# Products of values in tiles of 64 rows by 32 columns, into two banks of PSUM, beside two single score banks instead of three

## The chip, the cores and the metric

The kernel runs on one core of one Trainium2 chip. The metric is device time in microseconds (us) for one execution; a core's engines work side by side and wait for each other by semaphores. PE is the matmul engine (its weight loads are listed apart as PEld), ACT the scalar engine, DVE the vector engine, POOL the GpSimd engine, and SP issues most DMAs. Matmul results go to PSUM, which has eight banks of 128 partitions by 512 fp32 numbers each.

## What is computed

Two sublayers work on 2048 rows of 512 numbers, and a gate mixes them. Only the first, attention with 32 heads of 16 numbers each, matters for the change:

```python
q, k, v = qkv[0], qkv[1], qkv[2]
scores = einsum("bhqd,bhkd->bhqk", q, k) * Dh ** -0.5
p = softmax(scores, axis=-1)
o = einsum("bhqk,bhkd->bhqd", p, v)
a = o.transpose(0, 2, 1, 3).reshape(B, S, D) @ wo
out = g * a + (1 - g) * b
```

Here b is a Fourier sublayer (two products with DFT matrices along the features and along the rows), and g is a sigmoid of a weighted row sum.

## The kernel before

**The whole.** The order on every engine is written out by hand in the program. A front part (projections, the values `va`, most of the Fourier products) comes first; beside it go "scans", score products whose only use is the row maximum. Then follows the attention loop of 512 steps (lines 991 to 1039), and a short tail (from line 1045).

**A step of attention.** The 32 heads go as 16 pairs `p`. For each pair there are two halves `h` of 1024 queries and 16 blocks `kb` of 128 keys: 16 x 2 x 16 = 512 steps. A step makes scores for two heads (j = 0, 1) and two blocks of 512 queries (c = 0, 1), in fp32r (`qk`, line 204). The two heads of a call lie on rows 0 to 49 and 64 to 113 of the operands, so that their two products stand in the upper and the lower half of the array at the same time, with 128 columns each.

- c = 0 goes to a double bank, `wide1` (`qk_both`, line 229). One ACT instruction of 1024 numbers per partition makes the exponentials `eb` of both heads (line 234). There is one such double bank, so the next step's call waits until ACT has read it.
- c = 1 goes to two single banks (`qk_single`, line 237), from a rotation `order_` of three: d0, d1, k0. Two ACT instructions of 512 numbers make `e`, head 1 first (lines 241 and 242). Then line 243 swaps the last two names of the rotation. With three banks this gives head 1 the same bank in every step, while head 0 takes the other two in turn.
- The other double bank, `wide0`, belongs to what is done beside: in the first 300 steps a scan (line 135) whose maximum DVE takes at once (line 137), and later the rest of the Fourier and output products (line 185, "fill" here).

**The products of values** (`pv`, line 753) come one step later. The exponentials (128 keys by 512 queries) stream against 17 columns of `va`: 16 numbers of the head and a column of ones, which gives the sum for the softmax. Both are fp32, which the profile lists as two matmuls and two weight loads for each one of the program. Four tiles of 128 rows by 32 columns (`tile_position=(0, r)`) stand side by side in the array, one each for (c, j). All add into one bank, `pvb` (its tag is k1), over the 16 steps of a half. At the end of a half `quotients` (line 762) copies `pvb` to SBUF on DVE and sends the sums off; `divide` does the rest later. The next half's first product of values waits for that copy.

**The order on PE.** In the first 300 steps ("scan stage" here): scores c = 0, scan, scores c = 1, products of values of the step before. From step 301 (`MIX`, line 47; "fill stage") the products of two steps are made together in every second step. A period of two steps is then: scores c = 0 and c = 1, products of two steps, scores c = 0 and c = 1, fill products.

**PSUM.** `wide0` and `wide1` take two banks each, and the four tags d0, d1, k0, k1 one each: all eight banks are used.

**The tail** reads the last half out of `pvb` with two copies of 256 columns, one on DVE and one on ACT (lines 1050 and 1051), transposes them in the array, divides, and ends with the last output products; it uses the single banks too.

Of the kernel before, what the change touches and what calls it, by code (L numbers as in the profile page):

```python
# [24 lines left out]
NB = S // P  # L25
ND = D // P
NC = S // 512
VC = DH + 1
# [25 lines left out]
def build(tc, xT, wqkv, wo, wrT, wiT, cr, ci, gate, out):  # L54
    nc = tc.nc
    with ExitStack() as ctx:
# [21 lines left out]
        va = keep.tile([P, NB, H, VC], F32, name="va")  # L78
# [47 lines left out]
        def scan(n, ps):  # L126

            p, i = SEQ[n]
            qb, c = i // 4, i % 4
            qs, ks = scanned[p]  # L130
            if i == 0:
                new_maxima(p)
            for j in range(2):
                b = 64 * j
                nc.tensor.matmul(ps[:, j, :], qs[b:b + 48, qb * P:(qb + 1) * P],  # L135
                                 ks[b:b + 48, c * 512:(c + 1) * 512], start=True, stop=True)
            nc.vector.tensor_reduce(mx[p][:, :, qb, c], ps, axis=AX.X, op=ALU.max)  # L137
# [54 lines left out]
        def wide(i, name):  # L192
            return psf.tile([P, 2, 512], F32, tag=f"wide{i}", name=name)
# [16 lines left out]
                nc.tensor.matmul(pss[j], ks[b:b + 50, kb * P:(kb + 1) * P],  # L210
                                 qs[b:b + 50, q0:q0 + 512], start=True, stop=True)

        psk, order_ = [], ["d0", "d1", "k0"]

        def narrow(tag, name):
            return psk[0].tile([P, 512], F32, tag=tag, name=name)
# [6 lines left out]
        def next_eb():  # L223
            if len(both) < 4:
                both.append(ring4.tile([P, 2, 512], F32, tag="c", name="eb"))
            ebs[0] += 1
            return both[(ebs[0] - 1) % 4]

        def qk_both(p, h, kb):

            ps = wide(1 - SCANS_IN, "s3")
            qk(p, h, kb, 0, [ps[:, j, :] for j in range(2)])
            e = next_eb()
            nc.scalar.activation(e, ps, AF.Exp, scale=SCALE)  # L234
            return [e[:, j, :] for j in range(2)]

        def qk_single(p, h, kb, e):

            pss = [bank() for j in range(2)]
            qk(p, h, kb, 1, pss)  # L240
            for j in (1, 0):
                nc.scalar.activation(e[j], pss[j], AF.Exp, scale=SCALE)  # L242
            order_[-2:] = order_[-1], order_[-2]
            return e

        ebs, ahead, sums = [0], [], []
# [4 lines left out]
        with ExitStack() as pf:  # L251
# [381 lines left out]
            with ExitStack() as py:  # L633
# [13 lines left out]
                def go_ahead(k):  # L647

                    if k == 0:
                        assert seen[0] == FRONT, (seen, pace)  # L650
                        scanned.update(unfolded)
                        sums.append(narrow("k1", "pvb"))
                        nc.vector.memset(sums[0], 0.0)
                    if k == 1:
                        e = next_eb()
                        ahead.append(qk_single(0, 0, 0, [e[:, j, :] for j in range(2)]))
                    elif k == 2:
                        scan(seen[0], wide(1 - SCANS_IN, "s1"))
                        seen[0] += 1
                    else:  # L660
                        ahead.append(qk_both(0, 0, k // 3))
# [8 lines left out]
                for n, (ph, t, u) in enumerate(coef):  # L670
# [33 lines left out]
                    for w in range(CS):  # L704
                        s = u * CS + w
                        for i, (c_, a_) in enumerate(((hi, ah[s]), (hi, al[s]), (lo, ah[s]))):
                            halves_of(pss[t], c_[:, w, :], a_, s == 0 and i == 0, s == NB - 1 and i == 2)
                            beside()
                            if n >= len(coef) - NU and 3 * s + i in AHEAD:
                                go_ahead(AHEAD.index(3 * s + i))  # L710
                        if swap:
                            if 3 <= s < 8:
                                early[s + 5] = load_operand(1, s + 5, cp)
                            after(1 + 5 * (s % 8) + 4 * (s // 8), renew, s)
# [15 lines left out]
        with ExitStack() as pa:  # L730
# [1 line left out]
            cw = pa.enter_context(tc.tile_pool(name="cw2", bufs=2, reuse_waits="tile"))  # L732
            ap = pa.enter_context(tc.tile_pool(name="ap", bufs=1, reuse_waits="tile"))

            pvb = sums[0]
            rb = ap.tile([P, 512], F32, name="rb")
            nc.gpsimd.memset(rb, 1.0)

# [7 lines left out]
            def qk2(p, h, kb, c):  # L746
                if c == 0:
                    return qk_both(p, h, kb)
                n = turn1[0]
                turn1[0] += 1  # L750
                return qk_single(p, h, kb, [ring[n % len(ring)] for ring in single])

            def pv(p, h, kb, es):
                for c, j, r in quads:
                    nc.tensor.matmul(pvb[r:r + VC, :], va[:, kb, 2 * p + j, :], es[c][j],  # L755
                                     start=kb == 0, stop=kb == NB - 1, tile_position=(0, r))

            def bank2():
                ps = wide(1 - SCANS_IN, "s3")
# [2 lines left out]
            def quotients(p, h):  # L762
                ob = ap.tile([P, 512], F32, tag="ob", name="ob", bufs=2)
                nc.vector.tensor_copy(ob, pvb)  # L764
                lc = sm.tile([P, 16], F32, tag="lc", name="lc")
                for n, (c, j, r) in enumerate(quads):
                    nc.gpsimd.dma_start(lc[32 * n:32 * n + 32, :],  # L767
                                        ob[r + DH:r + VC, :].rearrange("p (s e) -> p s e", e=16))
                return p, h, ob, lc
# [189 lines left out]
            def part(t, *ks):  # L959

                if t not in groups:
                    if t in (3, 9):
                        ps = pair_banks()
                        groups[t] = ps[:, 0, :], ps[:, 1, :]
                    else:
                        groups[t] = bank2() if t == 8 else (bank(), pvb if t == 11 else bank())
                for k in ks:
                    mix_rest(t, groups[t], k, k == 0 or 7 < t < 11, k == 2)
# [5 lines left out]
            def flush():  # L974
                done = pend.pop(0)
                pv(*done)
                return done
# [13 lines left out]
            for step in range(NP * PERIODS):  # L991
                p, i = step // PERIODS, step % PERIODS
                h, kb = i // NB, i % NB
# [19 lines left out]
                es = ahead[2:] if step == 1 else [qk2(p, h, kb, 0)]  # L1013
# [18 lines left out]
                if done and done[2] == NB - 1:  # L1032
                    halved.append((step + (10 if done[0] < NP - 2 else 7 if done[0] < NP - 1 else 3), quotients(*done[:2])))
# [11 lines left out]
            halves_ = [slice(0, 256), slice(256, 512)]  # L1045
            blocks_ = [slice(s * P, (s + 1) * P) for s in range(4)]
            ob = ap.tile([P, 512], F32, tag="ob", name="ob", bufs=2)
            oh, ol = (cw.tile([P, 512], F32R, tag=tag, name=tag) for tag in ("chi", "clo"))
            direct[1].append((oh, ol))
            for c, copy in zip(halves_, (nc.vector.tensor_copy, nc.scalar.copy)):  # L1050
                copy(ob[:, c], pvb[:, c])
            part(3, 1)
            turned, spread = bank(), bank()
            for q in blocks_:
# [61 lines left out]
```

## Time and profile before

| what | value |
|---|---|
| median of 3 runs | 1726.87 us (1726.72 to 1727.06) |
| profiled execution, first to last instruction (span) | 1725.2 us |
| PE busy | 1713.5 us, 99% |
| ACT busy | 1506.8 us, 87% |
| DVE busy | 1089.1 us, 63% |
| POOL busy | 648.7 us, 38% |
| mean granted clock of PE | 0.999 |

Of the profiled execution only the span is given; it lies 1.7 us below the median of the runs, which count what lies around the instructions as well. Times within the trace are in us from the span's start. In a row of the timeline stand the start, how long the record (or the merged records) lasted, engine, line, operation, tiles as out<-in, shape (rows*columns for PE) and count; in brackets stands how long the engine had been idle before it, and what ended that. A record of PE lasts longer than the array is taken by it, since matmuls follow each other in a pipeline: it is the steps from start to start that add up. So PE's 99% doesn't say that the array streamed for 99% of the time.

### The profile page before, as it was taken

To read this page: it belongs to the slowest core of one execution; us is meant where nothing else is said; L and a number is where in the kernel's file an instruction comes from. 1 tells how busy PE (TensorE), PEld (TensorE's weight loads), DVE (VectorE), ACT (ScalarE), POOL (GpSimd) and SP (SyncE) were. 2 spreads that over 40 slices of the span, in tenths; PEclk is the share of its full clock that TensorE was granted. 3 is DMA by queue.
4 is the path that set the end of the run, shared out by engine and by line. 5 is a ranking of instruction groups with operands and counts; after the bars stand their busy time and mean duration, and the time that the engine had idled before them with its cause. 6 is when DMAs were issued, how large, how long until landed. Compare 5 with 4: busy or idle time off the path is not lost.

```text
span 1725.2 us, 36082 instructions
## 1 busy us (share of the span) xinstructions
PE 1713.5 (99%) x13680; PEld 1044.7 (61%) x13680; DVE 1089.1 (63%) x2059; ACT 1506.8 (87%) x2489; POOL 648.7 (38%) x770
## 2 busy tenths in 40 slices
PE   9999999999999999999999999999999999999998
PEld 7888888988888885333333333333455555555554
DVE  6898888999999996666666666666512212122333
ACT  6447889888888888999999999999988888888886
POOL 3672436655555762223233242322322322223222
PEclk9999999999999999999999999999999999999999
DMA  7783557534337663243323342351334244265712
GB/s 257 241 285 75 156 158 211 158 112 115 103 111 211 153 136 72 37 73 58 66 59 67 54 82 44 58 107 37 65 80 94 72 110 91 67 150 139 175 36 101
DMA packets 123710, 193.03 MB, mean 112 GB/s; under 512 B 54112, under 2 KB 56656, under 8 KB 116624
## 3 DMA queue, kind: packets, MB, share of 16 engines
q1 hardware_dynamic: 84464, 170.20, 37.7%
q0 software_dynamic: 38496, 19.47, 5.7%
q8 instruction: 107, 1.75, 0.4%
q10 hardware_dynamic: 576, 1.05, 0.2%
q14 instruction: 67, 0.55, 0.1%
HBM read 129.63 MB, written 61.61 MB: 111 GB/s over the span
## 4 chain that ended last, share of the span: by engine, by line
PE 96%; DVE 2%; DMA 1%; issue 1%; ACT 0%; SPq 0%; DVEq 0%; POOL 0%; ACTq 0%; POOLq 0%
PE pvb L755 29%; PE xy L185 25%; PE s L210 19%; PE s L185 9%; PE s L154 9%; PE s L135 5%; DVE fold L160 1%; DMA q_d<-eh 0%; DMA raws<-wqkv 0%; DMA ks<-kf_d 0%; PE s L554 0%; DVE y L853 0%; ACT fold L158 0%; DVE s L278 0%; DVE b L334 0%
## 5 line engine op out<-in xcount | busy, mean ns | idle before, releaser
L234 ACT ACTIVATE eb<-s 128x1024 f32<-128x1024 f32 x512 | 578.7, 1130 | 65.4 <-PE s L210 65.4
L242 ACT ACTIVATE e<-s 128x512 f32<-128x512 f32 x1022 | 608.9, 709 | 0.4 <-PE s L210 0.4
L137 DVE TENSOR_REDUCE mx<-s 128x2 f32<-128x1024 f32 x364 | 441.4, 1224 | 188.7 <-PE s L135 188.5
L755 PE MATMUL pvb<-eb,va 128*17 128x512 f32 x2052 | 513.0, 597 | 0.0
L755 PE MATMUL pvb<-e,va 128*17 128x512 f32 x2044 | 512.1, 597 | 0.0
L160 DVE CUSTOM_DVE_ANT_0 fold<-s,fold 128x512 f32<-128x512 f32 x660 | 443.9, 690 | 52.7 <-PE s L154 24.4
L158 ACT ACTIVATE fold<-s 128x512 f32<-128x512 f32 x660 | 389.9, 603 | 73.3 <-PE s L154 52.3
L210 PEld LDWEIGHTS s<-qs,ks 50*128 50x128 f32 x2048 | 214.9, 184 | 355.2 <-ACT eb L234 255.1
L210 PE MATMUL s<-qs,ks 50*128 50x512 f32 x2048 | 420.0, 434 | 0.0
L185 PE MATMUL xy<-b,c 64*128 64x512 f32 x2448 | 397.3, 392 | 0.3 <-ACT c L333 0.3
L154 PE MATMUL s<-ks,qs 48*128 48x512 f32 x1320 | 315.3, 405 | 1.6 <-DVE mx L160 1.0
L185 PEld LDWEIGHTS xy<-b,c 64*128 64x128 f32 x2448 | 283.9, 187 | 17.6 <-issue 1.0
L154 PEld LDWEIGHTS s<-ks,qs 48*128 48x128 f32 x1320 | 172.9, 184 | 47.0 <-DVE mx L160 12.5
L774 POOL DMA_DIRECT2D r_d<-lc x31 | 18.1, 583 | 456.4 <-DVE lc L773 456.4
L755 PEld LDWEIGHTS pvb<-eb,va 128*17 128x17 f32 x2052 | 70.5, 96 | 189.9 <-issue 182.7
L135 PE MATMUL s<-ks,qs 48*128 48x512 f32 x728 | 151.6, 394 | 0.7 <-DVE mx L137 0.7
L767 POOL DMA_DIRECT2D lc<-ob x124 | 62.9, 514 | 156.3 <-DVE ob L764 156.1
L185 PE MATMUL xy<-w,b 64*128 64x512 f32 x768 | 115.3, 392 | 0.0
L365 POOL TENSOR_TENSOR c<-craw,c 128x512 fp32r<-128x512 f32 x84 | 109.4, 1302 | 6.7
L185 PE MATMUL s<-b,chi 64*128 64x512 f32 x670 | 105.4, 391 | 0.0
L364 POOL CAST c<-craw 128x512 fp32r<-128x512 f32 x84 | 53.3, 635 | 125.1 <-PE xy L185 120.1
L871 DVE CAST chi<-craw 128x512 fp32r<-128x512 f32 x40 | 19.1, 477 | 111.4 <-PE s L185 99.3
(136 smaller groups left out, 1535.2 us busy)
## 6 DMA issues: line engine op xcount, KB each, us to landing
qs<-q_d SPq DMA_DIRECT2D x66, 256.0 KB
craw<-ci SPq DMA_DIRECT2D x64, 256.0 KB
craw<-cr SPq DMA_DIRECT2D x60, 256.0 KB
ks<-k_d SPq DMA_DIRECT2D x44, 256.0 KB
qs<-q_d SPq DMA_DIRECT2D x66, 128.0 KB
ab_d<-ab SPq DMA_DIRECT2D x32, 256.0 KB
y_d<-y SPq DMA_DIRECT2D x32, 256.0 KB
o_d<-oh POOLq DMA_DIRECT2D x28, 256.0 KB, 13.8
```

The lines of the kernel that those rows point to most:

```text
L135: nc.tensor.matmul(ps[:, j, :], qs[b:b + 48, qb * P:(qb + 1) * P], ks[b:b + 48, c * 512:(c + 1) * 512], start=True, stop=True)
L137: nc.vector.tensor_reduce(mx[p][:, :, qb, c], ps, axis=AX.X, op=ALU.max)
L154: nc.tensor.matmul(ps, qs[b:b + 48, qb * P:(qb + 1) * P], ks[b:b + 48, c * 512:(c + 1) * 512], start=True, stop=True)
L158: nc.scalar.activation(fold[j], ps, AF.Relu)
L160: nc.vector.tensor_tensor_reduce(out=fold[j], in0=ps, in1=fold[j], scale=1.0, scalar=-3.0e38, op0=ALU.add, op1=ALU.max, accum_out=mx[p][:, ...
L185: nc.tensor.matmul(ps[j], lhs[r], rhs[r], start=first, stop=last)
L210: nc.tensor.matmul(pss[j], ks[b:b + 50, kb * P:(kb + 1) * P], qs[b:b + 50, q0:q0 + 512], start=True, stop=True)
L234: nc.scalar.activation(e, ps, AF.Exp, scale=SCALE)
L242: nc.scalar.activation(e[j], pss[j], AF.Exp, scale=SCALE)
L365: sub(lo, raw, hi.bitcast(F32))
L755: nc.tensor.matmul(pvb[r:r + VC, :], va[:, kb, 2 * p + j, :], es[c][j], start=kb == 0, stop=kb == NB - 1, tile_position=(0, r))
L767: nc.gpsimd.dma_start(lc[32 * n:32 * n + 32, :], ob[r + DH:r + VC, :].rearrange("p (s e) -> p s e", e=16))
```

## The change

`pv` cuts each product in two by rows. Instead of four tiles of 128 rows by 32 columns there are eight of 64 rows by 32 columns: rows 0 to 63 (the first 64 keys) add into `pvb`, and rows 64 to 127 into a second bank `pvc`, so that each (c, j) has a tile in each half of the array. The program's products of values are twice as many. `pvc` takes the tag k0, which leaves the rotation: `qk_single` has two banks, d0 and d1. With the swap of line 243, head 0 of a step then takes the bank that head 1 had in the step before, and head 1 the bank that head 0 had, which ACT reads last. `quotients` adds `pvc` with a second DVE instruction, and the first product of the next half into `pvc` waits for that. At the start both banks are set to zero. In the tail ACT copies both parts of `pvb`, DVE adds `pvc` to each, and k0 then joins the rotation again.

```diff
-        psk, order_ = [], ["d0", "d1", "k0"]
+        psk, order_ = [], ["d0", "d1"]
...
-                        sums.append(narrow("k1", "pvb"))
-                        nc.vector.memset(sums[0], 0.0)
+                        for tag in ("k1", "k0"):
+                            sums.append(narrow(tag, "pvb"))
+                            nc.vector.memset(sums[-1], 0.0)
...
-            pvb = sums[0]
+            pvb, pvc = sums
...
             def pv(p, h, kb, es):
                 for c, j, r in quads:
-                    nc.tensor.matmul(pvb[r:r + VC, :], va[:, kb, 2 * p + j, :], es[c][j],
-                                     start=kb == 0, stop=kb == NB - 1, tile_position=(0, r))
+                    for b, sums_ in ((0, pvb), (64, pvc)):
+                        nc.tensor.matmul(sums_[r:r + VC, :], va[b:b + 64, kb, 2 * p + j, :], es[c][j][b:b + 64, :],
+                                         start=kb == 0, stop=kb == NB - 1, tile_position=(b, r))
...
                 nc.vector.tensor_copy(ob, pvb)
+                nc.vector.tensor_add(ob, ob, pvc)
...
-            for c, copy in zip(halves_, (nc.vector.tensor_copy, nc.scalar.copy)):
-                copy(ob[:, c], pvb[:, c])
+            for c in halves_:
+                nc.scalar.copy(ob[:, c], pvb[:, c])
+                nc.vector.tensor_add(ob[:, c], ob[:, c], pvc[:, c])
+            order_.append("k0")
```

## The prediction

> **What bounds the kernel now.** I read the page first: its busy shares, the chain that ended last, and the costliest groups.
>
> ```profile
> span 1725.2 us, 36082 instructions
> PE 1713.5 (99%) x13680; PEld 1044.7 (61%) x13680; DVE 1089.1 (63%) x2059; ACT 1506.8 (87%) x2489; POOL 648.7 (38%) x770
> ...
> PE pvb L755 29%; PE xy L185 25%; PE s L210 19%; PE s L185 9%; PE s L154 9%; PE s L135 5%; DVE fold L160 1%; DMA q_d<-eh 0%; DMA raws<-wqkv 0%; DMA ks<-kf_d 0%; PE s L554 0%; DVE y L853 0%; ACT fold L158 0%; DVE s L278 0%; DVE b L334 0%
> ...
> L242 ACT ACTIVATE e<-s 128x512 f32<-128x512 f32 x1022 | 608.9, 709 | 0.4 <-PE s L210 0.4
> ```
>
> The products of values (L755) have 29% of a chain that is nearly all PE, so they look like the place to save. But a chain names one engine where two are equally late, so I cut the span into stages: scan stage, fill stage with periods of one length, its last part, tail.
>
> ```profile
> 663.00:1237.00 574.00, 573.28 (x4237) 220.54 (x4235) 387.13 (x358) 571.10 (x904) 166.72 (x251) 1.00 0.32 61
> 1237.00:1593.00 356.00, 356.00 (x2929) 188.72 (x2926) 72.25 (x128) 317.50 (x490) 98.99 (x146) 1.00 0.42 101
> 1593.00:1708.00 115.00, 115.00 (x940) 61.37 (x939) 39.22 (x58) 94.17 (x143) 23.17 (x36) 1.00 0.39 101
> ```
>
> The columns are length, then busy time of PE, PEld, DVE, ACT, POOL. In the scan stage ACT is busy 571.10 of 574.00 us: PE and ACT are both full, so a faster PE gains nothing there. In the fill stage ACT has some 11% free and PE sets the pace. The front, 663 us, isn't touched. One step of the scan stage, PE and ACT:
>
> ```profile
> 1002.66 0.40 PE L135 MATMUL s<-ks,qs 48*128 48x512 f32 x2
> 1002.86 1.15 ACT L234 ACTIVATE eb<-s 128x1024 f32<-128x1024 f32 x1
> 1002.89 0.40 PE L210 MATMUL s<-qs,ks 50*128 50x512 f32 x2
> 1003.22 0.61 PE L755 MATMUL pvb<-eb,va 128*17 128x512 f32 x2
> 1003.23 0.61 PE L755 MATMUL pvb<-e,va 128*17 128x512 f32 x2
> 1003.66 0.60 PE L755 MATMUL pvb<-eb,va 128*17 128x512 f32 x2
> 1003.78 1.21 ACT L242 ACTIVATE e<-s 128x512 f32<-128x512 f32 x2
> 1004.20 0.50 PE L210 MATMUL s<-qs,ks 50*128 50x512 f32 x2
> 1004.54 0.40 PE L135 MATMUL s<-ks,qs 48*128 48x512 f32 x2
> 1004.74 1.17 ACT L234 ACTIVATE eb<-s 128x1024 f32<-128x1024 f32 x1
> ```
>
> On PE a pair of score products takes 0.23 (1002.66 to 1002.89), but 0.33 where the products of values follow (to 1003.22): 0.10 extra. Of these the first pass takes 0.44, the second 0.54 until the next scores: 0.10 extra. And the first scores take 0.34 until the scan instead of 0.23: their weights were not loaded ahead, 0.11. So going to the wide tiles and back costs 0.10 + 0.10 + 0.11 = 0.31 us, and this is what a change of tile shape could save. ACT meanwhile goes from `eb` to `eb` in 1.88 with no idle time in its rows.
>
> **The change part by part.**
>
> *Streaming.* Eight tiles of half the rows stream the same 512 columns in the same two passes: nothing is saved in the passes if all eight run at once. I cost the four more tiles of a pass at 0; the two records of a pass start 0.01 apart (1003.22, 1003.23), so if each further pair of tiles adds as much, it is up to 0.015 x 405 blocks = 6 us.
>
> *The switch between shapes.* Scores use 64 rows by 128 columns, and the products of values now 64 by 32: the row split stays, the column split changes. No row of the trace shows a switch of columns alone. One row shows a switch of rows alone, from transposes (128 by 128) to output products (64 by 128) in the tail:
>
> ```profile
> 1711.48 0.66 PE L1055 MATMUL s<-ident,ob 128*128 128x128 f32 x4
> 1712.06 0.30 PEld L185 LDWEIGHTS s<-b,chi 64*128 64x128 f32 x4 [0.17 <-issue]
> ```
>
> The weight load of the new shape waits for nothing that the profile shows, yet it starts only 0.08 before the last old record ends, and the two switches of both kinds above act alike. So one changed direction is enough for the pause, and I take it that the 0.31 stays (bounds: 0 and 0.31 saved). The Trainium skill, TensorEngine Tiling (Array Packing), Key Properties, says that a change of tiling mode drains the engine while a change of tile doesn't, and its list has 64x128 and 64x32 as two modes. By that rule nothing of the 0.31 goes and the sum is the one below; without it the sum would be that of rival 1. The row above agrees, though only for rows.
>
> *The third score bank.* Now the second score product of a step (head 1, c = 1) needs the bank that head 0 had a step before, which ACT reads last. Until now that wait did not exist. Behind it on PE stand the products of values, and behind these the next c = 0 scores that ACT needs. A closed loop arises. Its links come from the fill stage, where ACT isn't held up by itself:
>
> ```profile
> 1302.22 0.73 PE L210 MATMUL s<-qs,ks 50*128 50x512 f32 x4
> 1302.76 1.03 ACT L234 ACTIVATE eb<-s 128x1024 f32<-128x1024 f32 x1 [0.47 <-PE s L210]
> 1303.68 1.08 ACT L242 ACTIVATE e<-s 128x512 f32<-128x512 f32 x2
> 1304.17 0.65 PE L210 MATMUL s<-qs,ks 50*128 50x512 f32 x4
> 1304.75 0.61 PE L755 MATMUL pvb<-eb,va 128*17 128x512 f32 x2
> 1306.59 0.51 PE L210 MATMUL s<-qs,ks 50*128 50x512 f32 x2
> ...
> 1708.48 1.08 ACT L242 ACTIVATE e<-s 128x512 f32<-128x512 f32 x2
> 1709.61 0.12 PEld L755 LDWEIGHTS pvb<-e,va 128*17 128x17 f32 x4 [0.24 <-ACT e L242]
> ...
> L154 PEld LDWEIGHTS s<-ks,qs 48*128 48x128 f32 x1320 | 172.9, 184 | 47.0 <-DVE mx L160 12.5 <-ACT fold L158 7.5
> ```
>
> Scores c = 0 to the start of `eb`: 0.54 (1302.22 to 1302.76). From there to the end of the last `e`: 2.00 (1303.68 + 1.08 = 1304.76). From an ACT end to PE: 0.05 (1708.48 + 1.08 = 1709.56 to 1709.61). A weight load that stands behind a wait for a bank is held with its product (the L154 row: loads waited for DVE's and ACT's reads), so it is not hidden: 0.11 as above. I take it; without it the term is 0. Then 0.33 to the products of values.
>
> Scan stage: these take 0.98 (1003.22 to 1004.20). Loop over two steps: 0.54 + 2.00 + 0.05 + 0.11 + 0.33 + 0.98 = 4.01, or 2.005 a step.
>
> ```profile
> L234 ACT ACTIVATE eb<-s x290: 1024/1228/1255, 680.4 to 1229.5; 128x1024 f32<-128x1024 f32 x145
> L755 PE MATMUL pvb<-eb,va x648: 592/592/605, 1239.2 to 1590.4; 128*17 128x512 f32 x162
> L234 ACT ACTIVATE eb<-s x48: 1023/1026/1047, 1593.3 to 1707.6; 128x1024 f32<-128x1024 f32 x48
> ```
>
> Now a step takes (1229.5 - 680.4) / 289 = 1.900. So 0.105 x 300 steps = 31.5 us (15 without the weight load, 38 with the late tiles).
>
> Fill stage: the products of two steps take 1.84 (1304.75 to 1306.59). The loop runs once per period, since the scores made after the fill need the bank of those made before it: 0.54 + 2.00 + 0.05 + 0.11 + 0.33 + 1.84 = 4.87. A period now is 1306.59 - 1302.22 = 4.37, and there are 648 / 8 = 81 of them up to 1593. The 24 periods behind (48 `eb` in 114.3 us) are 9.4 us longer than 24 x 4.37; a long one has three fill pairs more, 3 x 0.23 = 0.69, so some 14 are long (5.06, over 4.87: no cost) and 9 short ones add to the 81. 90 x 0.50 = 45 us (35 without the weight load).
>
> *The end of a half.* DVE copies `pvb`, then adds `pvc`; the next half's first product of values waits for both.
>
> ```profile
> 1000.59 0.69 DVE L764 COPY ob<-pvb 128x512 f32<-128x512 f32 x1
>   PEld pvb L755: 6.9, 18
> L607 DVE TENSOR_TENSOR ab<-tx,xy 128x512 f32<-128x512 f32 x20 | 13.7, 683 | 0.0
> ```
>
> The second row says that in the scan stage's 18 halves PE already waits for the copy. An addition with one operand in PSUM is 0.68 (L607), and PE has no slack in the loop: 18 x 0.68 = 12 us (9 if ACT's stock of scores hides a part). Queued behind the addition on DVE is the scan's maximum (1.23 of a 2.0 step), which it delays without making DVE full. In the fill stage the next products come 4.37 - 1.84 = 2.5 us after the last ones, more than copy and addition: 0.
>
> *The ends.* One more memset at the start stands beside fill products: 0. In the tail ACT's and DVE's parts come after each other: 0.5 us.
>
> **Sum:** 31.5 + 12 + 45 + 0.5 = 89 on the span of 1725.2 gives 1814; what lies around it, 1.7 to the median of 1726.87, stays: **1816 us**, 5% slower. Its own range by the bounds is 1786 to 1827.
>
> **The rivals.**
>
> *1. The pauses go, since the row split stays.* Then 0.31 leaves each loop. Scan stage: 4.01 - 0.31 = 3.70, under ACT's 2 x 1.88, so a step stays at 1.90, and the ends of halves cost some 11. Fill stage: 4.87 - 0.31 = 4.56, still over 4.37: 90 x 0.19 = 17; the 14 long ones gain 0.31 each, -4. In all +24: 1751 us. If also the waiting weight load is hidden: 4.45, +7 in place of 17 and 3 less in the scan stage, 1738. If only 0.20 goes: 4.67, +27, -3, +13: 1764. So the gain of PE is eaten by ACT in one stage and by the lost bank in the other. For it: the rows show no switch of columns alone. Against it: the tail's switch. The Trainium skill (TensorE: Matmul & The Clock Gate, Part 3) says that a weight load overlaps a running matmul only where the row group differs; by that the 0.11 stays and this rival is 1764. The row of 1002.66 speaks against such a strict rule: PE goes on to the next pair on the same rows after 0.23, which leaves no room for 0.11 of load.
>
> *2. PE can't do eight tiles at once or can't issue them fast enough.* Instructions in a scan step rise from 28 to 44 (12 for scores and scan, 32 for values), in a period from 72 to 104. The fastest long stretch of the trace is a fill pair, 4 instructions in 0.23, 57 ns each. Were that a floor, a step would be 2.5 and a period 5.9, some +350: about 2080. Were upper and lower tiles to run one after the other, 0.86 more per block of values, some +430: about 2160. Against it: score pairs run on both halves at once, and four column tiles at once, but never both together.
>
> *3. Faster: a pass of 64 rows is shorter.* Score pairs of 64 rows go at 0.23 for 512 columns, values of 128 rows at 0.44 a pass. If it is the rows that make the difference and not the fp32 type, the block of two steps falls from 1.84 to about 1.0. The fill loop is then 4.87 - 0.84 = 4.0, 0.35 under now: 90 x -0.35 = -32; the long periods lose 0.84, -12; the scan stage stays with ACT, +5. In all -39: 1688 us. It decides from a pass under 0.32, where the fill loop falls below 4.37. No row speaks for rows against type.
>
> **How the numbers follow.** Forecast 57%, rival 1 25% (its lowest part nearly no change), rival 2 9%, rival 3 5%, and 4% that the lost bank costs nothing because ACT reads it in time. About 0.2% is what a measurement of this kernel tells from no change. So faster 5%, same 4%, slower 91%. Range 1737 to 1827 us: it takes in the forecast and rival 1 with the bounds of the unknown costs, and leaves out rivals 2 and 3 and most of the last case.
>
> **What would show it.** Right: in the scan stage ACT has idle time before `eb` and a step is near 2.0; PE's weight loads of L210 wait for `e` (L242); a period of the fill stage is near 4.9 and one with long fill stays near 5.07; 0.33 and 0.54 stand again around the products of values; the first products of a half come some 0.7 later behind the addition. Rival 1: scores follow the products of values after 0.43, the scan stage keeps 1.90. Wrong at the root: short periods under 4.37, or a pass other than 0.43 to 0.45.

## The result and the profile after

The changed kernel takes **1820.57 us** (median of 4 runs, 1820.19 to 1821.51) against 1726.92 us for the kernel before beside it: 93.7 us slower, a ratio of 1.0542 (95% interval 1.0527 to 1.0557). The forecast was 1816 us, range 1737 to 1827.

The page of the changed kernel, in the rows that answer to those shown of before:

```profile
span 1818.6 us, 44340 instructions
...
PE 1806.8 (99%) x17776; PEld 1081.9 (59%) x17776; DVE 1108.8 (61%) x2092; ACT 1525.7 (84%) x2490; POOL 649.9 (36%) x770
...
PE pvb L757 28%; PE xy L185 24%; PE s L210 22%; PE s L185 9%; PE s L154 9%; PE s L135 5%; DVE fold L160 1%; DMA raws<-wqkv 0%; ACT fold L158 0%; PE s L554 0%; DVE y L856 0%; SPq L524 0%; SPq L523 0%; DVE mx L160 0%; ACT ty L278 0%
```

PE is again 99% busy and again nearly the whole chain, so these rows alone tell of no new wait. What moved is the share of L210, the scores, from 19% to 22%: a record of PE that is held on the way counts as busy. The cut by stages, with its bounds moved to the same steps as before (length, then busy time of PE, PEld, DVE, ACT, POOL), says where the time went:

```profile
0.00:663.00 663.00, 658.83 (x5508) 568.00 (x5510) 584.64 (x1506) 519.25 (x946) 355.15 (x334) 1.00 0.58 163
663.00:1284.00 621.00, 620.30 (x6637) 248.35 (x6634) 399.31 (x376) 589.18 (x904) 167.43 (x251) 1.00 0.30 57
1284.00:1681.86 397.86, 397.86 (x4224) 197.58 (x4222) 76.98 (x138) 317.70 (x490) 99.03 (x146) 1.00 0.36 93
1681.86:1801.40 119.54, 119.54 (x1324) 62.35 (x1324) 41.30 (x61) 94.20 (x143) 23.24 (x36) 1.00 0.35 90
1801.40:1818.60 17.20, 10.23 (x92) 5.58 (x88) 6.61 (x13) 5.35 (x11) 5.08 (x4) 0.91 0.42 154
```

The front is untouched. The scan stage grew from 574 to 621 us, the fill stage from 356 to 398, its last part from 115 to 119.5, and the tail not at all. In the scan stage ACT now waits more. Its `eb` there, first in the kernel before, then in the changed one (busy time and mean ns, then the idle time before it):

```profile
L234 ACT ACTIVATE eb<-s 128x1024 f32<-128x1024 f32 x301 | 360.5, 1198 | 6.1 <-PE s L210 6.1
L234 ACT ACTIVATE eb<-s 128x1024 f32<-128x1024 f32 x301 | 308.6, 1025 | 35.0 <-PE s L210 19.8
```

The steps of the scan stage, by the start of `eb` in that stage, and two steps from the timeline (both banks of sums have the name `pvb` in the rows):

```profile
L234 ACT ACTIVATE eb<-s x292: 1024/1025/1042, 679.3 to 1278.2; 128x1024 f32<-128x1024 f32 x146
```

```profile
1010.29 0.39 PE L210 MATMUL s<-qs,ks 50*128 50x512 f32 x2
1010.62 0.62 PE L757 MATMUL pvb<-eb,va 64*17 64x512 f32 x4
1011.06 0.61 PE L757 MATMUL pvb<-eb,va 64*17 64x512 f32 x4
1011.18 1.08 ACT L242 ACTIVATE e<-s 128x512 f32<-128x512 f32 x2
1011.62 0.50 PE L210 MATMUL s<-qs,ks 50*128 50x512 f32 x2
1012.20 0.61 PE L210 MATMUL s<-qs,ks 50*128 50x512 f32 x2
1012.32 0.18 PEld L210 LDWEIGHTS s<-qs,ks 50*128 50x128 f32 x1 [0.17 <-ACT e L242]
1012.74 0.62 PE L757 MATMUL pvb<-eb,va 64*17 64x512 f32 x4
1013.75 0.50 PE L210 MATMUL s<-qs,ks 50*128 50x512 f32 x2
```

A step is (1278.2 - 679.3) / 291 = 2.058 on the mean, ends of halves included. Within it, short and long steps take turns: the products of values start at 1010.62, and 2.12 later at 1012.74. In the long step the score product of 1012.20 lasts 0.61 in place of 0.39, and the weight load of 1012.32 waits for `e`: this is the wait for the bank that ACT reads last (1011.18 + 1.08 = 1012.26). The pauses at the change of shape stand as before: 0.33 from scores to values (1010.29 to 1010.62), a first pass of 0.44, and 0.56 from the second pass to the next scores (1011.06 to 1011.62).

A period of the fill stage, by the scores behind the block of values, is 4.88 in place of 4.37:

```profile
1303.33 0.73 PE L210 MATMUL s<-qs,ks 50*128 50x512 f32 x4
1308.21 0.74 PE L210 MATMUL s<-qs,ks 50*128 50x512 f32 x4
```

### The profile page after: what moved, and what is told of

Read it like the earlier page. It is cut to its first block, busy times and chain, and to the rows that moved or that the text cites. A ratio compares the mean times of both kernels' runs of the same rounds, so it can differ in the third digit from the quotient of the medians.

```text
span 1818.6 us, 44340 instructions
## 1 busy us (share of the span) xinstructions
PE 1806.8 (99%) x17776; PEld 1081.9 (59%) x17776; DVE 1108.8 (61%) x2092; ACT 1525.7 (84%) x2490; POOL 649.9 (36%) x770
## 4 chain that ended last, share of the span: by engine, by line
PE 97%; DVE 2%; issue 1%; ACT 0%; DMA 0%; SPq 0%; DVEq 0%; POOL 0%; ACTq 0%; POOLq 0%
PE pvb L757 28%; PE xy L185 24%; PE s L210 22%; PE s L185 9%; PE s L154 9%; PE s L135 5%; DVE fold L160 1%; DMA raws<-wqkv 0%; ACT fold L158 0%; PE s L554 0%; DVE y L856 0%; SPq L524 0%; SPq L523 0%; DVE mx L160 0%; ACT ty L278 0%
## 5 line engine op out<-in xcount | busy, mean ns | idle before, releaser
L234 ACT ACTIVATE eb<-s 128x1024 f32<-128x1024 f32 x512 | 526.3, 1028 | 140.5 <-PE s L210 125.1
L242 ACT ACTIVATE e<-s 128x512 f32<-128x512 f32 x1022 | 554.5, 602 | 0.4 <-PE s L210 0.4
L757 PE MATMUL pvb<-eb,va 64*17 64x512 f32 x4104 | 528.6, 594 | 0.0
L757 PE MATMUL pvb<-e,va 64*17 64x512 f32 x4088 | 516.4, 594 | 0.0
L210 PEld LDWEIGHTS s<-qs,ks 50*128 50x128 f32 x2048 | 245.0, 184 | 425.4 <-ACT e L242 278.0
L210 PE MATMUL s<-qs,ks 50*128 50x512 f32 x2048 | 492.7, 447 | 0.0
L757 PEld LDWEIGHTS pvb<-eb,va 64*17 64x17 f32 x4104 | 78.4, 92 | 174.6 <-issue 157.7
L185 PEld LDWEIGHTS xy<-w,b 64*128 64x128 f32 x768 | 81.3, 186 | 10.6
## 6 DMA issues: line engine op xcount, KB each, us to landing
o_d<-oh POOLq DMA_DIRECT2D x28, 256.0 KB, 12.4
```

Source lines behind the costliest of these rows:

```text
L185: nc.tensor.matmul(ps[j], lhs[r], rhs[r], start=first, stop=last)
L757: nc.tensor.matmul(sums_[r:r + VC, :], va[b:b + 64, kb, 2 * p + j, :], es[c][j][b:b + 64, :], start=kb == 0, stop=kb == NB - 1, tile_posit ...
```

## The experiments

**The lost bank alone** (four tiles, two score banks):

```diff
-        psk, order_ = [], ["d0", "d1", "k0"]
+        psk, order_ = [], ["d0", "d1"]
...
                 copy(ob[:, c], pvb[:, c])
+            order_.append("k0")
```

> The kernel before, with its four tiles of 128 rows by 32 columns, but only two single score banks. Theory 'bank' (the lost bank closes a loop through ACT's last read): a scan step 2.0 in place of 1.90, a period of the fill stage 4.87 in place of 4.37, the long periods 5.07 as before; 31 + 45 us, so about 1803 us (1775 to 1806). Rival 'shape' (the eight tiles cost the time, by their number or by their starts; the lost bank is hidden): 1727 to 1735 us.

Measured: 1802.31 us against 1726.69, 75.6 us slower, ratio 1.0438 (1.0422 to 1.0454). Its `eb` rows in the scan stage, and one period of the fill stage:

```profile
L234 ACT ACTIVATE eb<-s x289: 1024/1025/1043, 680.6 to 1258.5; 128x1024 f32<-128x1024 f32 x145
```

```profile
1302.11 0.73 PE L210 MATMUL s<-qs,ks 50*128 50x512 f32 x4
1302.65 1.03 ACT L234 ACTIVATE eb<-s 128x1024 f32<-128x1024 f32 x1 [0.97 <-PE s L210]
1303.57 1.08 ACT L242 ACTIVATE e<-s 128x512 f32<-128x512 f32 x2
1304.70 0.18 PEld L210 LDWEIGHTS s<-qs,ks 50*128 50x128 f32 x1 [0.30 <-ACT e L242]
1305.13 0.61 PE L755 MATMUL pvb<-eb,va 128*17 128x512 f32 x2
1306.97 0.73 PE L210 MATMUL s<-qs,ks 50*128 50x512 f32 x4
```

A scan step is (1258.5 - 680.6) / 288 = 2.007 (2.005 was forecast). The period can be read link by link: scores to `eb` 0.54, `eb` to the end of the last `e` 2.00 (1303.57 + 1.08 = 1304.65), 0.05 to the weight load, 0.43 from there to the products of values (0.11 for the load and 0.33 were forecast). With the 1.84 of the products (1305.13 to 1306.97) that is 4.86, and so is the period (1302.11 to 1306.97). By the starts of `eb`, the first 300 steps grew by 31.8 us against the kernel before and the rest of the attention loop by 43.9; 31.5 and 45 were forecast. So four fifths of the slowdown come without a single tile changed.

**The second read at the end of a half**, added to the kernel with two banks, and to the kernel before:

```diff
                 nc.vector.tensor_copy(ob, pvb)
+                nc.vector.tensor_copy(ob, pvb)
```

> As the run with two banks and four tiles, and DVE reads the sums twice at the end of each half (a second copy of the same bank stands for the addition). Theory 'bank': 9 to 12 us above the run without the second read, all in the 18 halves of the scan stage; what is left to the changed kernel (0 to 8 us) is the price of eight tiles. Rival 'shape': within 3 us of the kernel before, and the changed kernel lies far above.

> The kernel before, three score banks and four tiles, with a second copy of the same bank on DVE at the end of each half. By the wait alone: 18 halves of the scan stage at up to 0.69, some 9 to 12 us above the kernel before, 1736 to 1739 us. If ACT's stock of scores hides a part when the third bank is there: 2 to 8 us. If the wait only costs where the loop through two banks leaves no slack: 0 to 2 us.

Measured: 1813.39 us with two banks, 11.1 above the run without the second read (ratio to before 1.0502, 1.0487 to 1.0518). With three banks 1739.16 us, 12.5 above the kernel before (1.0072, 1.0057 to 1.0087). The wait by itself would be 18 x 0.69 = 12.4 us, so a stock of scores hides at most a small part of it, with or without the third bank. What waited for the second copy in the kernel with three banks, from its source view (us, times):

```profile
L765 DVE COPY ob<-pvb x31: 690/691/692, 697.9 to 1687.2; 128x512 f32<-128x512 f32 x31
...
  POOL lc L768: 174.0, 31
  PEld pvb L755: 20.0, 18
  PE pvb L755: 12.5, 18
```

Of 31 halves PE waits at 18, all those of the scan stage, 12.5 us in all: 0.69 for each, the whole length of the copy.

**The changed kernel without the addition:**

```diff
                 nc.vector.tensor_copy(ob, pvb)
-                nc.vector.tensor_add(ob, ob, pvc)
```

> The changed kernel without the addition of the second bank at the end of a half; this leaves the second half of each block of keys out of the result. Theory 'bank': 9 to 12 us under the changed kernel, 1808 to 1812 us, from the scan stage alone. Rival 'shape': no change, 1820 us, as the addition would stand beside other work.

Measured: 1808.96 us, 11.6 under the changed kernel (ratio to before 1.0477, 1.0459 to 1.0494).

**What is left to the tiles.** The changed kernel against two banks with two reads is the step from four tiles to eight with nearly all else alike: 1820.57 - 1813.39 = 7.2 us, or 0.018 for each of 406 blocks of values. That 75.6 + 11.1 + 7.2 = 93.9 comes near the 93.7 measured proves nothing, since the runs lie on one path from the kernel before to the changed one. The other order tests it: without the second read in both, eight tiles against four cost 1808.96 - 1802.31 = 6.7 us, and the read 11.6. So the parts hardly depend on each other.

**The price of a change of shape, by itself.** A small kernel runs 40 rounds of each pattern (one execution):

```python
for _ in range(40):
    scores()                 # fp32r, two products of 64 rows x 128 columns
    tiles(rows, cols, m)     # fp32, products that fill the array in another shape
```

> None of the reference's work: 40 rounds each of a pair of fp32r products (64 rows by 128 columns, 512 columns of data) followed by fp32 products in another shape, with no waits for other engines. A round that switches nothing (64 by 128 after 64 by 128) should take 0.23 + 0.86 = 1.09 us. If any change of shape costs the pause (forecast): 1.09 + 0.31 = 1.40, less for a shorter weight load, for 64 by 32, 128 by 32, 64 by 64 and 128 by 128 after the pair alike, and for 128 by 32 after 128 by 128. If only a change of rows pauses (rival 1): 64 by 32 and 64 by 64 after the pair, and 128 by 32 after 128 by 128, take 1.09 to 1.12, and the others 1.3 to 1.4.

Rows of its timeline, two rounds of each pattern, in order: fp32 in the same shape (64 by 128); 64 by 32; 128 by 32; 64 by 64; 128 by 128; then scores over all 128 rows (L41) with 128 by 32 and, last, with 128 by 128, the same shape again.

```profile
50.04 0.80 PE L38 MATMUL s<-xr,wr 64*128 64x512 f32 x1
51.13 0.80 PE L38 MATMUL s<-xr,wr 64*128 64x512 f32 x1
...
100.58 0.50 PE L38 MATMUL s<-xr,wr 64*128 64x512 f32 x2
102.02 0.50 PE L38 MATMUL s<-xr,wr 64*128 64x512 f32 x2
...
140.66 0.50 PE L38 MATMUL s<-xr,wr 64*128 64x512 f32 x2
142.08 0.50 PE L38 MATMUL s<-xr,wr 64*128 64x512 f32 x2
...
200.56 0.50 PE L38 MATMUL s<-xr,wr 64*128 64x512 f32 x2
202.00 0.50 PE L38 MATMUL s<-xr,wr 64*128 64x512 f32 x2
...
250.05 0.49 PE L38 MATMUL s<-xr,wr 64*128 64x512 f32 x2
251.53 0.49 PE L38 MATMUL s<-xr,wr 64*128 64x512 f32 x2
...
310.07 0.50 PE L41 MATMUL s<-xr,wr 128*128 128x512 f32 x1
311.48 0.49 PE L41 MATMUL s<-xr,wr 128*128 128x512 f32 x1
...
370.54 0.79 PE L41 MATMUL s<-xr,wr 128*128 128x512 f32 x1
371.62 0.79 PE L41 MATMUL s<-xr,wr 128*128 128x512 f32 x1
```

From start to start: 1.09 and 1.08 in one shape throughout, and 1.44, 1.42, 1.44, 1.48, 1.41 with a change there and back. Rows kept and columns changed (64 by 32, 64 by 64, and 128 by 32 after 128 by 128) cost as much as rows changed or both. The Trainium skill's rule (TensorEngine Tiling (Array Packing), Key Properties: a change of tiling mode drains the engine) agrees with every pair of shapes tried here, at 0.33 to 0.39 us for there and back. Rival 1 is refuted. Eight tiles of 64 by 32 also take 0.02 more than four of 128 by 32 (1.44 to 1.42), near the 0.018 of the kernel, and all eight do run at once: their round would otherwise be near 2.3.

**Is it ACT's last read, or a fixed delay?** Half of head 0's exponentials for c = 1 left out, so that the last read ends earlier while each wait stays in place. The first form set the tiles' other half to ones beforehand:

```diff
             for j in (1, 0):
-                nc.scalar.activation(e[j], pss[j], AF.Exp, scale=SCALE)
+                n = 512 if j else 256
+                nc.scalar.activation(e[j][:, 0:n], pss[j][:, 0:n], AF.Exp, scale=SCALE)
```

> Two score banks and four tiles, and head 0's exponentials of c = 1 (the read of a bank that comes last) made for 256 of the 512 queries only; the rest of that tile keeps ones, so those results are left out. By rows of the run with two banks the instruction gets some 0.21 us shorter (0.605 for 512 numbers, 1.03 for 1024). Theory 'loop through the last read': the fill stage's period falls by that, 4.87 to 4.66, and a scan step from 2.01 to 1.90; about 1750 us in all (1744 to 1758). Rival 'any wait for the bank costs a fixed delay at PE' (the semaphore and the weight load, not ACT's end): periods stay at 4.87 and the time at 1795 to 1802 us.

> The control: the same shorter exponentials in the kernel before with three banks (the same results left out). Fill stage paced by PE: periods stay at 4.37. Scan stage: ACT no longer limits, PE needs 1.88 a step by its own links (0.33 + 0.98 + 0.34 + 0.23), so 1.88 to 1.89 in place of 1.90: 3 to 6 us under the kernel before, 1721 to 1724 us. If PE was not also full in the scan stage: far less than that, down to 1700 us.

Measured: 1758.51 us with two banks, just past the far end of what was expected, and 1727.73 with three, which fits neither expectation (1.0004, 0.9995 to 1.0013). The trace of the second shows a fault of the experiment: the memsets sat behind other work on POOL, and ACT's first short exponentials waited for them.

```profile
671.57 0.52 POOL L739 MEMSET rb<- 128x512 f32 x1
672.03 1.46 POOL L745 MEMSET e<- 128x512 f32 x3
672.59 0.38 ACT L243 ACTIVATE e<-s 128x256 f32<-128x256 f32 x1 [4.30 <-POOL e L745]
```

So both went again with the first five made in full and no memsets (`n = 512 if j or made[0] < 6 else 256`).

> As the run with two banks and shorter exponentials (half of head 0's for c = 1 left out), but the first five are made in full instead of setting their tiles to ones before; the memsets had held up the first steps of attention by some 5 us in both runs, behind other work on POOL. Loop through the last read: about 1753 us, with a scan step of 1.90 and a period of 4.65. Fixed delay: 1795 to 1802 us.

> The control with three banks, in the same manner (the same results left out). PE as full as ACT in the scan stage: 1721 to 1724 us. PE with room there: under 1715 us.

Measured: 1752.81 us (1.0149, 1.0134 to 1.0164) with two banks, 1722.88 (0.9979, 0.9970 to 0.9989) with three. A period of the run with two banks, by its score products after the block of values, and the exponentials between:

```profile
1303.98 0.73 PE L210 MATMUL s<-qs,ks 50*128 50x512 f32 x4
1304.52 1.03 ACT L234 ACTIVATE eb<-s 128x1024 f32<-128x1024 f32 x1 [1.01 <-PE s L210]
1305.44 0.87 ACT L244 ACTIVATE e<-s 128x512 f32<-128x512 f32 x2
1306.79 0.61 PE L757 MATMUL pvb<-eb,va 128*17 128x512 f32 x2
1308.63 0.74 PE L210 MATMUL s<-qs,ks 50*128 50x512 f32 x4
```

The pair of exponentials takes 0.87 in place of 1.08, and the period 4.65 in place of 4.86: the loop shrinks by just what its ACT link lost. The price of the lost bank falls from 75.6 to 1752.81 - 1722.88 = 29.9 us. A scan step, from the starts of `eb`, is (1231.8 - 679.6) / 290 = 1.904 with two banks and (1223.6 - 680.2) / 288 = 1.887 with three. So the control gains only 4 us although ACT's work per step fell by about a tenth: PE was nearly as full as ACT in the scan stage.

## Why the prediction was right, step by step

- *The scan stage is full on two engines, the fill stage on PE alone.* Shown for PE: taking ACT time away from the kernel before gave 4 us. That a faster PE would gain nothing in the scan stage rests on ACT's 571.10 of 574.00 us; no run tried it.
- *The pause stays with the rows kept.* Shown by the kernel's own 0.33 and 0.56, and for each pair of shapes by the small kernel. This was the choice between forecast and rival 1, and before the run only a switch of rows alone could be read.
- *The third bank, 31.5 + 45 = 76.5 us.* Measured 75.6 by itself, 31.8 and 43.9 by stages. Scan step 2.007 for 2.005, period 4.86 for 4.87, weight load included. In the last part, by the starts of every second `eb`, the short periods went from 4.37 to 4.86 and the long ones stayed at 5.07, as said. That it is a loop through ACT's last read is shown by the shorter exponentials. The weight load's 0.11 was not tried apart; it is read from the rows of a period alone.
- *The end of a half, 12 us.* Measured 11.1, 11.6 and 12.5 in three surroundings; nothing in the fill stage, as said.
- *Eight tiles at 0, up to 6 us.* Measured 7.2 and 6.7: the one term that was set too low by more than 1 us. The intervals of the two ratios are some 0.0015, or 2.6 us, to each side, so whether it lies beyond its bound isn't shown. The later starts of more tiles were the guess; the runs show 0.02 a block, not why.
- *The tail at 0.5 us.* From the start of the last `eb` to the end of the span it is 17.7 us in the changed kernel and 17.6 before: nothing that the rows can tell.
- *What would show it:* ACT's idle time before `eb` was to be seen in the scan stage. It was there, 35.0 us against 6.1, though this is less than the 47 us that the stage grew (see the last section). The wait of L210's weight loads for `e` was there, though in every second step only: the loop spans two steps, so one of two carries the wait. Rivals 2 and 3 are out: the passes are 0.44, and all eight tiles run in them.

## What to carry to other kernels

When a buffer is taken from a rotation, follow the new wait around: what stands behind the waiting instruction on its engine, who needs that, and when that one's last read frees the buffer. If this closes a loop, its sum over the steps it spans is the new period, and each link can be read from the old trace; here that gave 75.6 us to within one. The smaller tile, which kept one side of the shape, bought nothing on its own here: look first at which engine would take the saved time, and at whether the pause depends on that side at all.

## What the runs showed of the hardware that was not expected

- ACT with no time left showed longer records. Its `eb` has a median of 1228 ns in the scan stage of the kernel before and 1025 ns in that of the changed kernel, for the same work. Where ACT is full, an instruction starts well before the record of the one ahead ends: in the kernel before, the `eb` of 1002.86 lasts to 1004.01, and the next instruction starts at 1003.78. Where PE makes ACT wait, the record shrinks, so only part of the room shows as idle time: 28.9 of the 47 us that the scan stage grew.
- Loading weights for the same rows of the array that a product is using added nothing that shows while the shape stayed: a round over all 128 rows takes 1.08 (370.54 to 371.62), with a weight load for each product. The Trainium skill (TensorE: Matmul & The Clock Gate, Part 3) lists weight loads as overlapping with a running matmul only where the row group differs, while its text above the list also lets a load into the background weight buffer run ahead. This round fits the second and speaks against the first, though no run leaves the loads out. Only behind a change of shape (0.34 in place of 0.23 in the kernel before), or behind a wait for the product's own bank (0.43 in place of 0.33), did the load show, with some 0.1.
